# A gated FNet block on one core: the order of the side jobs around the first MLP1 units, earlier bias copies and an earlier load for MLP2, and one closing addition on GpSimd

## The chip, the cores and the metric

The kernel runs on one core of a Trainium2 chip. The metric is the device time of one execution in microseconds. Three runs of the kernel before are given, and one more execution was profiled.

## The reference

The input `x` has 2048 rows of 512. It is normalised by rows, goes through a Fourier mixing (real part of a two-sided DFT) and, beside that, through a two-layer MLP with squared ReLU; the MLP's output is passed through SiLU and gates the Fourier part, and `x` is added.

```python
xn = _layernorm(x)
a = jnp.einsum("bsd,ed->bse", xn, dft_hid_re)
b = jnp.einsum("bsd,ed->bse", xn, dft_hid_im)
s = jnp.einsum("ts,bse->bte", dft_seq_re, a) - jnp.einsum("ts,bse->bte", dft_seq_im, b)
h = jnp.einsum("bsd,df->bsf", xn, w1) + b1      # F = 1792
h = jnp.maximum(h, 0) ** 2
g = silu(jnp.einsum("bsf,fd->bsd", h, w2) + b2)
return x + s * g
```

## The kernel before

Every large product is in fp32 accuracy: an operand is split into a high part (`split_hi`, a copy on ScalarE, L125) and a low part (`split_lo`, a subtraction on VectorE, L128), and three matmuls, high·high, high·low and low·high, make one product (`PASSES`). On top of that, blocks of 2 by 2 are multiplied with seven products instead of eight (`PRODUCTS`), so each operand also needs sums of its blocks (`sums_a`, `sums_b`: three VectorE instructions, L257 to L269) ahead of the split. A tile's preparation is therefore a load (a DMA issued by SyncE, SP), sums on VectorE, a high split on ScalarE and a low split on VectorE.

The order on every engine is the order in which the Python code issues the instructions; nothing reorders them. The preparations are generators: each name such as `V6` or `x3` stands for one tile, and every mention of it in a table makes `go` run that tile's next step. The names that matter here: `x0` to `x7` are the token tiles of MLP1 (`tokens`: load, normalisation with two L610 instructions, sums, splits), `V2` to `V6` the first-layer weights that are made in place (`make_w1`: load, sums, splits), `m` the rows of statistics, `w` the second-layer weights (`make_w2`), `l4` and `l5` loads of second-layer weights, `h` the operands of MLP2 (`operand`: load, sums, splits), `y` and `p` operands and weights of the Y stage.

The stages follow each other on TensorE:

- up to 98 us: the sequence DFT of chunks 0 and 1 (`products`), whose results leave the four banks `pq1` through `last_out`;
- up to 335 us: chunks 2 to 7, 8 steps (c, j) of 42 matmuls each (L325). `EARLY` names the side steps behind each (c, j);
- up to 413 us: the Y stage, eight `YUnit`s with the hidden DFT (L704). `Y_SIDE` names two lists of side steps for each unit;
- up to 562 us: MLP1, 28 `HUnit`s H0 to H27 (L704), seven for each quarter c of the tokens. H6, for example, uses the weight of `V6`, and from H7 on the tiles `x2` and `x3` are used;
- up to 702 us: MLP2, 28 steps n of 42 matmuls (`outer`, L810), the first of them laid into H27, and the gate with the output.

In an `HUnit` the order on TensorE is: its product 1, the products 5 and 4 of the unit before, its products 7 and 6, product 3 of the unit before, its product 2. Product 3 goes into the bank (region B) in which product 5 lay, so it waits until VectorE has read that (`c22`, L774). `H_SIDE` gives three lists of side steps: the first is issued ahead of product 1, the second behind `c21` of the unit before, the third at the end. A side step on VectorE that stands in the first list thus stands ahead of `c22` in VectorE's queue, and one in the second list behind it. On VectorE a unit's own work is L774 twice and L789.

At the start of MLP2 two bias copies (`bias`, on ScalarE) put `b2` into the banks of products 2 and 4. In step n of MLP2 the operand `h(n+3)` gets its sums and then `h(n+2)` its split. `h2`, `h3` and all later operands lie in a buffer of the rotation `u` (three buffers, also used by the results of MLP1) or in `wd0`.

The tail computes the last quarter's four blocks, C11, C22, C12, C21: bias and sums of the products (`step`, L1035), SiLU on ScalarE, a product with the Fourier part (`times`, L857), an addition of `x` (`plus`, L862) and the store.

Of the kernel before, what the change touches and what calls it, by code (L numbers as in the profile page):

```python
# [11 lines left out]
ALU = mybir.AluOpType  # L12

P = 128
S, D, F = 2048, 512, 1792
NS, ND, NF = S // P, D // P, F // P
NJ, NP = NS // 2, NF // 2
# [3 lines left out]
NTC = S // TC  # L21
# [19 lines left out]
}  # L41

# [6 lines left out]
    (("x0",), ("k1",)),  # L49
    (("x1",), ()),  # L50
    (("V2", "x1", "x1", "m1"), ("x1", "V3", "x2")),
    (("x0", "x0", "V2", "V4", "V3"), ("x1", "x1", "x2")),
)


H_SIDE = {
    0: ((), ("V2",), ()),
    1: (("V4",), ("V3",), ("V5", "x3")),
    2: (("x2",), ("V4",), ("V6",)),
    3: (("V5",), ("V5",), ()),  # L60
    4: (("V6",), ("V6",), ("w4",)),
    5: ((), ("x2", "x3", "m2"), ("x4",)),
    6: (("x3",), ("x3",), ("x5",)),
    7: (("w4",), ("w4",), ("w5",)),
    8: ((), ("x4",), ()),
    9: (("x4",), ("x4",), ("x6",)),
# [10 lines left out]
    22: (("w1",), ("h0",), ("w2",)),  # L77
    23: ((), ("h1",), ("w3",)),
    24: (("w2",), ("w1",), ("w6", "h2")),
    25: (("w3",), ("w2",), ("l4",)),  # L80
    26: (("w6",), ("w3",), ("l5", "h3")),
    27: (("h2",), (), ()),
}
ACT_PAIR = (7, 10, 13, 15, 17, 18, 19, 20, 26)
O_SIDE = {0: (("h4",), ("h5",)), 1: ((), ("w6",))}
# [28 lines left out]
C21, C11, C22, C12 = range(4)  # L114
# [5 lines left out]
def fnet_gated_kernel(ctx, tc, x, xt, ct, wd, w1, w2, b1, b2, out):  # L120
    nc = tc.nc
# [8 lines left out]
    def split(*parts):  # L130
        split_hi(*parts)
        split_lo(*parts)

    def copy(to, src, scale=1.0):
        nc.scalar.activation(to, src, AF.Copy, scale=scale)
# [19 lines left out]
    def bank(tag, name):  # L155

        return acc.tile([P, 512], F32, tag=tag, name=name)

    def buf(tag, shape, name, dtype=F32):
        bufs = {"u": 3, "bn": 3, "sm": 3}.get(tag, 1)  # L160
        return pool.tile(shape, dtype, tag=tag, bufs=bufs, name=name)
# [109 lines left out]
    def sums_rows(t, r, turned=False):  # L271

        sums_a(t, r[:, C12:C12 + 1], r[:, C11:C22 + 1], r[:, C11], r[:, C21], turned)
# [75 lines left out]
    def go(*names):  # L349


        for v in names:
            if v[0] == "h" and int(v[1:]) >= NTC * NP:
                continue
            if v not in making:
                making[v] = makers[v[0]](int(v[1:]))
            next(making[v])
# [177 lines left out]
    def last_out(k, op):  # L535
        to = last.rearrange("p (h i m d t) -> p h d m i t", h=2, i=2, m=2, d=2)[:, k // 2, k % 2]
        op(to, accs[1][k].rearrange("p (m i t) -> p m i t", m=2, i=2))

    for k in range(3):
        last_out(k, nc.vector.tensor_copy)  # L540


    closing = None
    for n, s in enumerate(steps):
        c, j = s
        if j == 0:
            ms = {k: bank(tag, f"m{k}_{c}") for k, tag in
                  {1: "bb", 2: "b20", 6: "b21", 3: "b30", 5: "b31", 7: "b32", 4: ("ba", "bc")[c % 2]}.items()}
# [23 lines left out]
        if j == NJ - 1:  # L572
            e = buf("e", [P, 2048], f"c{c}")
# [9 lines left out]
    xT, W1, W2, fin, ready = {}, {}, {}, {}, {}  # L583
# [82 lines left out]

    def operand(n):

        if n < 2:
            x_, t = (buf(f"pq{n}{i}", [P, 4, 256], f"hr{n}_{i}") for i in range(2))  # L670
        else:
            e = buf("u" if n % 4 else "wd0", [P, 8, 256], f"hr{n}")
            x_, t = e[:, 4:8], e[:, 0:4]
        nc.sync.dma_start(x_, HD[divmod(n, NP)])
        yield
        sums_rows(t, x_)
        yield
        g = ready[n] = buf(("xc6", "xc7", "xc4")[n % 3], [P, 2, 7, 256], f"g{n}", F32R)
        for s, src in ((slice(0, 4), t), (slice(4, 7), x_[:, 0:3])) if n < 2 else ((slice(0, 7), e[:, 0:7]),):
            split(g[:, HI, s], g[:, LO, s], src)  # L680
        yield

# [5 lines left out]
    class Unit:  # L688

        def __init__(self, n):  # L690
            self.n = n
            self.at = {}
# [105 lines left out]
    def bias(m, n, cols=slice(0, 2)):  # L798

        m = m.rearrange("p (k e) -> p k e", k=2)[:, cols]  # L800
        b = BIASED[n] * 256
        copy(m, b2s[:, None, b:b + 256].to_broadcast([P, cols.stop - cols.start, 256]))
# [14 lines left out]
    def at(src, k):  # L817

        h, b = WHERE[k]
        return src.rearrange("(h k p) (b e) -> h b p k e", h=2, k=2, b=2)[h, b]  # L820
# [34 lines left out]
    def times(c, e, k, cols=slice(0, 2)):  # L855
        w = slice(cols.start * 256, cols.stop * 256)
        nc.vector.tensor_tensor(e[:, k, w], e[:, k, w], fin[c][k // 2][:, k % 2, w], op=ALU.mult)  # L857

    def plus(c, e, k, cols=slice(0, 2)):
        w = slice(cols.start * 256, cols.stop * 256)  # L860
        z = e[:, k, w]
        nc.vector.tensor_tensor(z, z, fin[c][2 + k // 2][:, k % 2, w], op=ALU.add)  # L862
        nc.sync.dma_start(at(out[c * TC:(c + 1) * TC], k)[:, cols], z.rearrange("p (k e) -> p k e", e=256))

    go("m0")
# [23 lines left out]
    for u in range(1, NC):  # L889
        n = 2 * u + 2  # L890
# [26 lines left out]
        before = unit  # L917


    for n in range(NTC * NP):  # L920
        unit = HUnit(n)
        first, second, later = H_SIDE.get(n, ((), (), ()))
        go(*first)
        unit.products(1)
        unit.seed("B", "A")
        before.c11()
        before.products(5)
        before.c22()
        before.products(4)
        before.c21()  # L930
        go(*second)
        unit.products(7)
        unit.m7()
        unit.products(6)
        unit.seed("C", "B")
        before.products(3)
        before.c12()
        unit.products(2)
        before.square()
        go(*later)  # L940
        before = unit

    class Banks(dict):

        def __init__(self, c):
            self.c = c

        def __missing__(self, k):
            tag = {1: "bb", 2: "b20", 6: "b21", 4: ("ba", "bc", "ba")[self.c], 7: ("bc", "b32", "b32")[self.c],
                   5: "b30", 3: "b31"}[k]  # L950
            self[k] = bank(tag, f"m{k}_o{self.c}")
            return self[k]

    ms = Banks(0)
    bias(ms[2], 2)
    bias(ms[4], 4)
    outer(ms[1], 1, 0)
    before.c11()
    before.products(5)
# [12 lines left out]
    for n in range(NTC * NP):  # L972
        c, p = divmod(n, NP)
        last = c == NTC - 1
        if n and not last and p == 0:

            ms = Banks(c)
            for k in (2, 4, 5):
                bias(ms[k], k)
        elif last and p == 0:  # L980

            ms = {k: bank(t, f"m{k}_last") for k, t in
                  {1: "b20", 2: "b21", 6: "b30", 7: "b31", 5: "bb", 3: "ba"}.items()}
            m4 = bank("bc", "m40_last"), bank("b32", "m41_last")
            bias(ms[5], 5)
            bias(m4[0], 4, slice(0, 1))
            bias(ms[2], 2)
            bias(m4[1], 4, slice(1, 2))

        def add(k, p):  # L990
            if last and k == 4:
                for i in range(2):
                    outer(m4[i], k, NP * c + p, (i,))
            else:
                outer(ms[k], k, NP * c + p)

        go(*O_SIDE.get(n, ((), ()))[0])
        if n == 1:
            for k, i in ((1, 1), (2, 1), (6, 1), (4, 1), (5, 0), (3, 0), (7, 1), (5, 1), (3, 1)):
                add(k, i)  # L1000
        elif n and (not last or p < REST):
            for k in ORDER if p else FIRST_LAST if last else FIRST:
                add(k, p)
        if n == 1:

            nc.scalar.activation(stats[:, 0, 0, 0:1], stats[:, 0, 0, 0:1], AF.Silu)
        go(f"h{n + 3}")
        if p == NP - 1 and not last:
            e = buf("e", [P, 4, 512], f"z{c}")
            list(combine(lambda k: halves(e[:, k]), ms))  # L1010
            done_next = c, e
        if c and not last and p in (3, 4):
            put(*done, p - 1)
        go(f"h{n + 2}", *O_SIDE.get(n, ((), ()))[1], f"h{n + 6}")
        if p == (3 if last else 5):
            load_fin(c)
        if p == NP - 1 and not last:
            done = done_next
        elif c:
            for k in ((2, 3), (0,), (1,), (), (), (), ())[p] if not last else ((), (0,), (1,), (2,), (3,), (), ())[p]:  # L1020
                finish(*done, k)


    e = buf("u", [P, 4, 512], f"z{c}")
    tail = NP - 1
    whole = slice(0, 512)
    w = [slice(i * 256, (i + 1) * 256) for i in range(2)]
# [6 lines left out]
    def step(to, a, b, op, w=whole):  # L1034
        nc.vector.tensor_tensor(e[:, to, w], a[:, w], e[:, b, w], op=op)  # L1035
# [25 lines left out]
    for f in range(REST, NP):  # L1061
        outer(m4[1], 4, NP * c + f, (1,))
    times(c, e, C12)
    step(C21, m4[1], C21, ALU.subtract, w[1])
    silu(e, C21, two)
    times(c, e, C21, one)
    plus(c, e, C21, one)
    times(c, e, C21, two)
    plus(c, e, C21, two)
    plus(c, e, C12)  # L1070


def _launch(arrays, out_shape):
# [40 lines left out]
```

## Time and profile before

| what | value |
|---|---|
| three runs | 708.91, 710.57, 710.85 us; median 710.57 us |
| profiled execution, own time | 709.49 us |
| profiled execution, span of its instructions | 707.7 us |
| TensorE busy with matmuls | 696.0 us (98%), 5440 matmuls |
| VectorE busy | 607.6 us (86%) |
| ScalarE busy | 357.0 us (50%) |
| granted TensorE clock | 0.999 |

The page of the profile gives busy time by engine, the chain of work that ended last and the costliest groups of instructions. The timeline lists instructions with their start, their duration and, in brackets, the idle time of the engine ahead of them and what ended it. "x12" means that twelve instructions of one kind that followed each other are merged into the row. Matmuls are pipelined: one lasts some 280 ns in the profile, while the next begins after 118 ns.

### The profile page before, as it was taken

Reading aid. Unit: us, or ns where it says so; the run is one execution under the profiler, and the core shown is the slowest. Engines: PE = TensorE matmul, PEld = TensorE weight load, DVE = VectorE, ACT = ScalarE, POOL = GpSimd, SP = SyncE. Lnnn points to the kernel's source line nnn. Section 1 sums busy time; section 2 is a strip of 40 time slices with the busy share of each in tenths; the row PEclk is TensorE's granted clock in tenths of the full one; section 3 lists DMA queues with packets and bytes.
Section 4 is the critical chain, followed back from the end, with each engine's and each line's share of the span. In section 5 each row is a group of like instructions: output and inputs, shape, how many; then the busy total and the mean of one; then the engine's idle time right before and its main releaser. Section 6 shows DMA issues by size and latency. Waiting matters only on the chain.

```text
span 707.7 us, 13133 instructions
## 1 busy us (share of the span) xinstructions
PE 696.0 (98%) x5440; PEld 671.6 (95%) x5440; DVE 607.6 (86%) x850; ACT 357.0 (50%) x471; POOL 5.2 (1%) x8
## 2 busy tenths in 40 slices
PE   9999999999999999999999999999999999999996
PEld 6778889999999999999999999999999999999996
DVE  7999779999989887888899699999649489989896
ACT  4446534444433333353455457677778754444441
POOL 0000000000000000000000000000000000101000
PEclk9999999999999999999999999999999999999999
DMA  8535755667575545286588444687426855767743
GB/s 302 189 112 188 280 193 206 244 225 266 189 273 211 181 145 179 90 283 229 176 294 273 155 167 161 215 338 259 163 114 221 316 184 192 188 204 191 238 151 119
DMA packets 50619, 146.88 MB, mean 208 GB/s; under 512 B 4864, under 2 KB 19200, under 8 KB 49152
## 3 DMA queue, kind: packets, MB, share of 16 engines
q1 hardware_dynamic: 43264, 126.13, 52.4%
q10 hardware_dynamic: 6208, 18.88, 6.8%
q0 software_dynamic: 1088, 1.05, 1.0%
q8 instruction: 42, 0.69, 0.4%
q14 instruction: 17, 0.14, 0.1%
HBM read 99.88 MB, written 46.15 MB: 206 GB/s over the span
## 4 chain that ended last, share of the span: by engine, by line
PE 90%; DVE 5%; ACT 2%; DMA 1%; issue 1%; ACTq 0%; DVEq 0%; SPq 0%
PE m L325 32%; PE m_o L810 14%; PE r_B L704 13%; PE r_A L704 8%; PE pq_b L340 7%; PE m_last L810 5%; PE r_C L704 4%; PE r_D L704 4%; PE pq_bb L340 1%; PE pq_ba L340 1%; PE pq_bc L340 1%; DMA hr<-hd 1%; DVE g L128 1%; DVE yg L128 1%; DVE c L306 1%
## 5 line engine op out<-in xcount | busy, mean ns | idle before, releaser
L325 PEld LDWEIGHTS m<-g,xc 128*128 128x128 f32 x2016 | 236.4, 188 | 1.3 <-DVE g L128 0.6
L325 PE MATMUL m<-g,xc 128*128 128x256 f32 x2016 | 237.0, 280 | 0.7 <-DVE g L128 0.4
L125 ACT ACTIVATE g<-u 128x1792 fp32r<-128x1792 f32 (+3 forms) x70 | 100.1, 1430 | 145.6 <-PE m L325 76.8
L128 DVE TENSOR_TENSOR g<-u,g 128x1792 fp32r<-128x1792 f32 (+3 forms) x70 | 117.5, 1679 | 26.7 <-ACT g L125 26.5
L810 PE MATMUL m_o<-w,g 128*128 128x256 f32 x882 | 106.1, 282 | 1.4 <-DVE g L128 1.0
L810 PEld LDWEIGHTS m_o<-w,g 128*128 128x128 f32 x882 | 105.5, 191 | 1.8 <-DVE g L128 1.2
L125 ACT ACTIVATE g<-hr 128x1792 fp32r<-128x1792 f32 (+2 forms) x30 | 47.9, 1603 | 50.7 <-PE m_o L810 31.2
L704 PE MATMUL r_B<-xT,w 128*128 128x256 f32 x504 | 69.6, 282 | 1.3 <-DVE h L774 1.3
L340 PE MATMUL pq_b<-g,xc 128*128 128x512 f32 x240 | 66.8, 397 | 0.3 <-ACT xc L125 0.2
L704 PEld LDWEIGHTS r_B<-xT,w 128*128 128x128 f32 x504 | 64.2, 190 | 1.5 <-DVE h L774 1.5
L128 DVE TENSOR_TENSOR g<-hr,g 128x1792 fp32r<-128x1792 f32 (+2 forms) x30 | 56.7, 1894 | 3.2 <-ACT g L125 3.2
L340 PEld LDWEIGHTS pq_b<-g,xc 128*128 128x128 f32 x240 | 43.8, 188 | 13.2 <-ACT xc L125 2.4
L704 PE MATMUL r_A<-xT,w 128*128 128x256 f32 x336 | 45.5, 283 | 0.6 <-DVE xT L128 0.6
L704 PEld LDWEIGHTS r_A<-xT,w 128*128 128x128 f32 x336 | 42.2, 190 | 1.2 <-DVE xT L128 1.0
L704 PE MATMUL r_B<-wdp,yg 128*128 128x256 f32 x288 | 37.5, 283 | 0.2 <-DVE y L714 0.2
L704 PEld LDWEIGHTS r_B<-wdp,yg 128*128 128x128 f32 x288 | 35.6, 190 | 0.6 <-DVE y L714 0.4
L810 PE MATMUL m_last<-w,g 128*128 128x256 f32 x294 | 35.3, 282 | 0.0
L810 PEld LDWEIGHTS m_last<-w,g 128*128 128x128 f32 x294 | 35.2, 191 | 0.0
L257 DVE TENSOR_TENSOR u<-u 128x512 f32<-128x512 f32 x48 | 32.9, 685 | 0.7 <-DMA u<-in_ct 0.7
L128 DVE TENSOR_TENSOR yg<-yraw,yg 128x1792 fp32r<-128x1792 f32 x13 | 26.2, 2022 | 5.5 <-ACT yg L125 5.4
L306 DVE TENSOR_TENSOR c<-m,c 128x512 f32<-128x512 f32 x42 | 27.2, 685 | 1.8 <-PE m L325 1.0
L125 ACT ACTIVATE yg<-yraw 128x1792 fp32r<-128x1792 f32 x13 | 22.1, 1700 | 6.7 <-DVE yraw L266 5.2
(171 smaller groups left out, 863.5 us busy)
## 6 DMA issues: line engine op xcount, KB each, us to landing
u<-in_ct SPq DMA_DIRECT2D x63, 512.0 KB, 3.6
hd<-h ACTq DMA_DIRECT2D x28, 512.0 KB, 4.4
hr<-hd SPq DMA_DIRECT2D x28, 512.0 KB, 3.7
wdp<-wdd SPq DMA_DIRECT2D x8, 896.0 KB, 7.3
yraw<-pqd SPq DMA_DIRECT2D x13, 512.0 KB, 4.7
pqd<-c SPq DMA_DIRECT2D x6, 1024.0 KB, 4.3
y<-y ACTq DMA_DIRECT2D x8, 512.0 KB, 5.0
fin<-y SPq DMA_DIRECT2D x16, 256.0 KB, 4.6
```

Source lines behind the costliest of these rows:

```text
L125: nc.scalar.activation(hi, src, AF.Copy)
L128: nc.vector.tensor_tensor(lo, src, hi.bitcast(F32), op=ALU.subtract)
L257: nc.vector.tensor_tensor(t[:, 0:2], r[:, 0:1].to_broadcast([P, 2, 256]), r[:, 1:3], op=ALU.add)
L306: nc.vector.tensor_tensor(part_(to), m, part_(frm), op=op)
L325: nc.tensor.matmul(ps[:, d], w[:, a_, d * P:(d + 1) * P], halves(mv(b_)), start=first and d == 0 and (a_, b_) == (HI, HI), stop=last and ( ...
L340: nc.tensor.matmul(accs[c][k], w, part[c, j][:, b_, 2 * h:2 * h + 2], start=j == 0 and h == 0 and (a_, b_) == (HI, HI), stop=j == NJ - 1 a ...
L704: nc.tensor.matmul(self.region(REGION[k]), w, mv, start=i == 0 and k in (1, 7), stop=i == len(ops) - 1, skip_group_check=True)
L810: nc.tensor.matmul(m[:, i * 256:(i + 1) * 256], ready[n][:, a_, H_SLOT[a], i * P:(i + 1) * P], W2[p][:, b_, b], start=p == 0 and i == 0 an ...
```

## The change

- `last_out` for chunk 1: of three copies that VectorE made in the order 0, 1, 2, two (2 and 0) go to ScalarE, ahead of its next split, and VectorE keeps 1.
- `EARLY`: the splits of `y0` and `y1` are issued one step (c, j) later, and with them the load of `y2`.
- `Y_SIDE`: in the last Y unit `x1` is split ahead of the sums of `V2`, and the sums of `V3` follow the load of `V4`.
- `H_SIDE`: in H0 to H6 the sums of `x2`, `V5`, `V6` and the normalisation and sums of `x3` move from the first lists to the second ones or to other units. `V6` is split in H5 instead of H4, `x2` in H4 instead of H5; `x3` is loaded one unit earlier, ahead of `V5`; the loads of `m2`, `x4` and `w4` move too.
- MLP2: the bias copies for products 2 and 4 are issued in H27 ahead of ScalarE's square of H26; `h3` is loaded one unit earlier, ahead of `l4` and `l5`, into a buffer pair of its own (`pq00`, `pq01`); the split of `h2` stands ahead of the sums of `h3`.
- Tail: the addition of `x` for block C12 goes from VectorE, where it was last, to GpSimd, directly behind its product; its store is then issued ahead of those of C21.

```diff
-    (7, 1): ("p2",), (7, 2): ("p2", "y0"), (7, 3): ("y0", "y2", "p3"), (7, 4): ("p3", "y1"), (7, 5): ("y1",),
+    (7, 1): ("p2",), (7, 2): ("p2",), (7, 3): ("y0", "p3"), (7, 4): ("y0", "y2", "p3"), (7, 5): ("y1", "y1"),
...
-    (("x0", "x0", "V2", "V4", "V3"), ("x1", "x1", "x2")),
+    (("x0", "x0", "x1", "x1", "V2"), ("V4", "V3", "x2")),
...
-    0: ((), ("V2",), ()),
-    1: (("V4",), ("V3",), ("V5", "x3")),
-    2: (("x2",), ("V4",), ("V6",)),
-    3: (("V5",), ("V5",), ()),
-    4: (("V6",), ("V6",), ("w4",)),
-    5: ((), ("x2", "x3", "m2"), ("x4",)),
-    6: (("x3",), ("x3",), ("x5",)),
+    0: ((), ("V2", "x2"), ("x3",)),
+    1: (("V4",), ("V3",), ("V5",)),
+    2: ((), ("V4", "V5"), ("V6",)),
+    3: ((), ("x3", "V5"), ("m2",)),
+    4: ((), ("V6", "x2"), ("x4",)),
+    5: ((), ("V6", "x3"), ("w4",)),
+    6: ((), ("x3",), ("x5",)),
...
-    25: (("w3",), ("w2",), ("l4",)),
-    26: (("w6",), ("w3",), ("l5", "h3")),
+    25: (("w3",), ("w2",), ("h3", "l4")),
+    26: (("w6",), ("w3",), ("l5",)),
...
-    for k in range(3):
-        last_out(k, nc.vector.tensor_copy)
+    for k, op in ((2, copy), (0, copy), (1, nc.vector.tensor_copy)):
+        last_out(k, op)
...
-        if n < 2:
-            x_, t = (buf(f"pq{n}{i}", [P, 4, 256], f"hr{n}_{i}") for i in range(2))
+        apart = n in (0, 1, 3)
+        if apart:
+            x_, t = (buf(f"pq{n % 3}{i}", [P, 4, 256], f"hr{n}_{i}") for i in range(2))
...
         before.c12()
+        if n == NTC * NP - 1:
+            ms = Banks(0)
+            for k in (2, 4):
+                bias(ms[k], k)
         unit.products(2)
         before.square()
...
-    bias(ms[2], 2)
-    bias(ms[4], 4)
...
+        if not n:
+            go("h2")
         go(f"h{n + 3}")
...
-        go(f"h{n + 2}", *O_SIDE.get(n, ((), ()))[1], f"h{n + 6}")
+        go(*[f"h{n + 2}"][:n], *O_SIDE.get(n, ((), ()))[1], f"h{n + 6}")
...
     times(c, e, C12)
+    plus(c, e, C12, eng=nc.gpsimd)
     step(C21, m4[1], C21, ALU.subtract, w[1])
...
     plus(c, e, C21, two)
-    plus(c, e, C12)
```

More of the change, by code (lines that the diff above doesn't have):

```diff
@@ L678, in operand @@
         g = ready[n] = buf(("xc6", "xc7", "xc4")[n % 3], [P, 2, 7, 256], f"g{n}", F32R)
-        for s, src in ((slice(0, 4), t), (slice(4, 7), x_[:, 0:3])) if n < 2 else ((slice(0, 7), e[:, 0:7]),):
+        for s, src in ((slice(0, 4), t), (slice(4, 7), x_[:, 0:3])) if apart else ((slice(0, 7), e[:, 0:7]),):
             split(g[:, HI, s], g[:, LO, s], src)
@@ L857, in times, with plus @@
         nc.vector.tensor_tensor(e[:, k, w], e[:, k, w], fin[c][k // 2][:, k % 2, w], op=ALU.mult)
-    def plus(c, e, k, cols=slice(0, 2)):
+    def plus(c, e, k, cols=slice(0, 2), eng=None):
         w = slice(cols.start * 256, cols.stop * 256)
         z = e[:, k, w]
-        nc.vector.tensor_tensor(z, z, fin[c][2 + k // 2][:, k % 2, w], op=ALU.add)
+        (eng or nc.vector).tensor_tensor(z, z, fin[c][2 + k // 2][:, k % 2, w], op=ALU.add)
         nc.sync.dma_start(at(out[c * TC:(c + 1) * TC], k)[:, cols], z.rearrange("p (k e) -> p k e", e=256))
@@ L917, in fnet_gated_kernel, with __init__, __missing__ @@
         before = unit
+    class Banks(dict):
+        def __init__(self, c):
+            self.c = c
+        def __missing__(self, k):
+            tag = {1: "bb", 2: "b20", 6: "b21", 4: ("ba", "bc", "ba")[self.c], 7: ("bc", "b32", "b32")[self.c],
+                   5: "b30", 3: "b31"}[k]
+            self[k] = bank(tag, f"m{k}_o{self.c}")
+            return self[k]
     for n in range(NTC * NP):
@@ L941, in fnet_gated_kernel @@
         before = unit
[L943 to L954, printed above, removed]
-    bias(ms[2], 2)
-    bias(ms[4], 4)
     outer(ms[1], 1, 0)
```

## The prediction

> **What bounds the kernel now.** I read the page first, then TensorE's waits, then the timeline around each wait.
>
> ```profile
> PE 696.0 (98%) x5440; PEld 671.6 (95%) x5440; DVE 607.6 (86%) x850; ACT 357.0 (50%) x471; POOL 5.2 (1%) x8
> ...
> L325 PE MATMUL m<-g,xc 128*128 128x256 f32 x2016 | 237.0, 280 | 0.7 <-DVE g L128 0.4
> ```
>
> TensorE (PE) is the bound; the change takes no matmul away, so all it can win are PE's stops and the tail behind the last matmul. The second row gives the size of a stop: 2016 matmuls in 237.0 us are one each 0.118 us, but one lasts 0.28 in the profile, so that an idle time in the rows is understated by 0.16. The longest stops with a releaser (their idle time, how many, the longest):
>
> ```profile
> PE r_B L704 <- DVE h L774: 1.3, 1, 1.3
> ...
> PE m_o L810 <- DVE g L128: 1.0, 1, 1.0
> PE r_A L704 <- DVE xT L128: 0.6, 1, 0.6
> ```
>
> These three, and three shorter ones whose rows stand below, belong to places that the change edits. Behind a stop the second matmul also comes late: six of them take 0.98 us at 450.39 (row below), as against the 0.87 of others, so 0.1 more. A stop costs its idle time, 0.16 and 0.1.
>
> **Copies of chunk 1 (`last_out`).**
>
> ```profile
> 98.42 1.88 DVE L537 COPY plain<-pq_b 128x512 f32<-128x512 f32 x3
> 98.67 1.71 ACT L125 ACTIVATE g<-u 128x1792 fp32r<-128x1792 f32 x1 [3.81 <-DVE u L259]
> ...
> 100.45 5.73 PE L325 MATMUL m<-g,xc 128*128 128x256 f32 x47 [0.29 <-DVE plain L537]
> ...
> 105.88 2.02 DVE L128 TENSOR_TENSOR g<-u,g 128x1792 fp32r<-128x1792 f32 x1 [0.39 <-ACT g L125]
> ```
>
> PE waits for the third of three VectorE copies, that of bank 2. ScalarE (ACT) has sat idle 3.81 us ahead of 98.67, so two copies fit there before its split, and VectorE's single one ends near 99.1, ahead of its use. The stop of 0.29 + 0.16 + 0.1, about 0.53, goes. What is late next: the low split at 105.88 follows VectorE's own chain and ends at 107.90 whatever PE does; PE, 0.5 earlier, wants it near 107.84 and stands some 0.15. Gain **0.4** (0.2 to 0.53).
>
> **The Y operands in `EARLY`.**
>
> ```profile
> 311.32 0.96 DVE L128 TENSOR_TENSOR yg<-yr,yg 128x768 fp32r<-128x768 f32 x1 [1.47 <-ACT yg L125]
> ...
> 313.72 2.02 DVE L128 TENSOR_TENSOR g<-u,g 128x1792 fp32r<-128x1792 f32 x1
> ...
> 315.79 4.47 PE L325 MATMUL m<-g,xc 128*128 128x256 f32 x36 [0.37 <-DVE g L128]
> ```
>
> The half split of `y0` (0.96) stands on both engines ahead of the split of g(7,4), for which PE stops. Behind it, g ends near 314.2, before PE's 315.2. The moved work is 4 half splits within some 15 us in which every step leaves VectorE about 1 us; the load of `y2` waits until 320.4, is needed at 329, and holds one load of `p3` on SP for less than a microsecond, which is used at 335. Gain 0.37 + 0.16 + 0.1 = **0.6** (0.4 to 0.65).
>
> **Y7 and H0 to H6.** Here the answer is not the stop that goes, but VectorE's queue.
>
> ```profile
> 406.89 2.08 DVE L128 TENSOR_TENSOR xT<-x0e,xT 128x768 fp32r<-128x768 f32 x2
> 408.89 0.69 DVE L263 TENSOR_TENSOR w1raw<-w1raw 128x512 f32<-128x512 f32 x1
> ...
> 410.41 0.68 DVE L263 TENSOR_TENSOR w1raw<-w1raw 128x512 f32<-128x512 f32 x1
> ...
> 412.08 0.88 PE L704 MATMUL r_A<-xT,w 128*128 128x256 f32 x4
> ...
> 413.56 0.50 PE L704 MATMUL r_A<-xT,w 128*128 128x256 f32 x2 [0.61 <-DVE xT L128]
> ...
> 414.64 2.48 DVE L610 TENSOR_TENSOR xr<-xr,rows 128x1024 f32<-128x1024 f32 x2
> ...
> 417.04 0.42 DVE L714 TENSOR_TENSOR y<-r_B,y 128x256 f32<-128x256 f32 x1
> ...
> 417.90 2.02 DVE L128 TENSOR_TENSOR w<-w1raw,w 128x1792 fp32r<-128x1792 f32 x1
> ...
> 419.83 0.69 DVE L263 TENSOR_TENSOR w1raw<-w1raw 128x512 f32<-128x512 f32 x1
> ...
> 427.21 0.48 DVE L774 SCALAR_TENSOR_TENSOR h<-r_B,b1s,h 128x256 f32<-128x256 f32 x1
> ...
> 428.92 2.02 DVE L128 TENSOR_TENSOR w<-w1raw,w 128x1792 fp32r<-128x1792 f32 x1
> ...
> 444.64 1.59 PE L704 MATMUL r_A<-xT,w 128*128 128x256 f32 x12
> ...
> 450.39 0.98 PE L704 MATMUL r_B<-xT,w 128*128 128x256 f32 x6 [1.32 <-DVE h L774]
> ...
> 452.57 0.30 PEld L704 LDWEIGHTS r_A<-xT,w 128*128 128x128 f32 x2 [0.23 <-DVE xT L128]
> ```
>
> H0 starts at 412.08 and stands four matmuls later, until 413.56: 1.0 + 0.1 = 1.1. In the changed order the splits of `x1` run on VectorE at 408.89, where the weight sums are now, and that goes whole. The stop in H6 (1.32 + 0.16 + 0.1 = 1.6) is `c22`, held in VectorE's queue behind the normalisation and sums of `x3`; with the 0.3 at 452.57 (low split of `x3`) 3.0 stands to be won.
>
> But the same work has to pass VectorE. Its costs from start to next start are: split pair of a token tile 2.00 (408.89 − 406.89), weight or token sums 1.52 (410.41 − 408.89), normalisation 2.40 (417.04 − 414.64), Y7's two 0.86 (417.90 − 417.04), weight split 1.93 (419.83 − 417.90), a unit's own three 1.71 (428.92 − 427.21). From 408.89 the changed queue is: `x1` split, two weight sums, `x2` normalisation, Y7's two, `V2` split, `x2` sums, `V4` sums, H0's three, `V3` split: 2.00 + 3.04 + 2.40 + 0.86 + 1.93 + 1.52 + 1.52 + 1.71 + 1.93 = 16.9, to 425.8. Then four units' three, `V4`, `V5` splits, `V5`, `V6` sums, `x3` normalisation, `x2` split: 6.84 + 3.86 + 3.04 + 2.40 + 2.00 = 18.1, to 443.9. There the split of `V6` begins; it ends at 446.0 (2.02).
>
> H6 needs that split: its product 1 takes the low part of `V6` at the third matmul. H6 starts in the second half of the row at 444.64, at 445.36; 1.1 earlier that is 444.25, its third matmul 444.5. So a new stop of 1.5 + 0.1 stands at H6's start, where before only `c22` waited; part of it may fall on H5's product 3, without a change in the sum. Even with no backlog the split of `V6` would be late: it follows `c22` of H4 in H5's list and leaves VectorE about 0.3 too late. Behind it `c22` of H5 and the `x3` split pass in time. Net 3.0 − 1.6 = **1.4** (0.5, if VectorE idles a microsecond for a load; 2.6, if no backlog forms).
>
> The loads moved here: `x3`'s load waits on SP for Y7's store, and `V5`'s and `V6`'s loads stand behind it (rival 2).
>
> **Start of MLP2.**
>
> ```profile
> 559.34 1.12 ACT L135 ACTIVATE m_o<-b2s 128x512 f32<-128x512 f32 x2 [0.40 <-ACT h L793]
> ...
> 560.00 1.69 PE L810 MATMUL m_o<-w,g 128*128 128x256 f32 x12 [0.44 <-ACT m_o L135]
> ...
> 564.49 1.71 ACT L125 ACTIVATE g<-hr 128x1792 fp32r<-128x1792 f32 x1 [0.40 <-ACT h L793]
> ...
> 567.79 0.69 DVE L263 TENSOR_TENSOR hr<-hr 128x512 f32<-128x512 f32 x1 [6.99 <-DMA hr<-hd]
> ...
> 569.32 2.02 DVE L128 TENSOR_TENSOR g<-hr,g 128x1792 fp32r<-128x1792 f32 x1
> ...
> 571.40 28.82 PE L810 MATMUL m_o<-w,g 128*128 128x256 f32 x239 [0.95 <-DVE g L128]
> ```
>
> The bias copies (1.12) go ahead of the square of H26, whose 1.06 us and store then lie between: ScalarE reaches them at 557.8, PE needs the first at 559.4. The stop of 0.44 + 0.16 + 0.1 = 0.7 goes; the delayed store is that of an operand used 28 units on. At 571.40 PE waits for the low split of `h2`, which stood in VectorE's queue behind the sums of `h3`; those idled 6.99 us for a load. With `h2` first, the split can run at 566, behind its high half (564.49 + 1.71, 0.7 earlier), and PE wants it at 569.6: 0.95 + 0.16 + 0.1 = 1.2 goes. What is late next, `h3`, has its load moved from behind `l5` to ahead of `l4`, 16 us earlier, and PE needs it at 574.6, two microseconds behind its split. Gain **1.9** (1.2 to 1.9).
>
> **Tail.**
>
> ```profile
> 703.39 1.03 DVE L862 TENSOR_TENSOR z<-z,fin 128x256 f32<-128x256 f32 x2
> ...
> 639.15 1.21 POOL L845 DMA_DIRECT2D z<-in_x  x1 [28.84 <-DVE z L857]
> ...
> out<-z SPq DMA_DIRECT2D x5, 256.0 KB, 2.1
> ...
> out<-z SPq DMA_DIRECT2D x2, 128.0 KB, 1.7
> ```
>
> VectorE's last two additions end at 704.42; without C12's 0.68 the last ends near 703.8, and the last store is then one of 128 KB (1.7 to landing) instead of 256 KB (2.1): up to 0.9 less. No row shows an addition on GpSimd (POOL). From below it is VectorE's 0.68; from above I put 2.2, near twice POOL's 1.21 for another kind. C12's product is done at 701.9; with 1.2 its store leaves at 703.2 and the later ones behind it in time (0.9). With 2.2 they queue behind it on SP, and the gain is gone (−0.3). Whether POOL's addition stops VectorE's four of 0.42 that run in the same time, no row shows either: with 1.2 that eats the 0.9. I take the middle of 0 and 0.9, **0.4** (−1.0, with 2.2 and stopping, to 0.9).
>
> The Trainium skill speaks against the edit twice. "SBUF — State Buffer", section "SBUF: two separate sides", states that GpSimd and VectorE share one port pair, locked for a whole instruction, and that a VectorE operation with two SBUF inputs is blocked by a GpSimd one that reads SBUF. By that rule the edit is worth 0 instead of 0.4 and the sum 0.4 less. No run shows it so far. "GPSIMD Engine Reference", section "Instruction dispatch", states some 6 us for the first call of freshly loaded code; that is rival 3.
>
> **Sum.** 0.4 + 0.6 + 1.4 + 1.9 + 0.4 = 4.7 us. The profiled execution took 709.49, 1.08 below the median of the three runs; the four times average 709.96, and from that I take the 4.7: 705.3 us.
>
> **Rivals.**
>
> 1. VectorE stays the bound through H0 to H6 and something in it, such as a load, gives back that stage's 1.4 and the tail: 0.4 + 0.6 + 1.9 − 0.4 = 2.5, 707.5 us. For it: the queue has no idle time from 408.89 to 446. Against: loads there landed long before use. Chance 0.12.
>
> 2. Slower. `x3`'s load is issued when Y7's store has landed, and `V5`'s load behind it.
>
> ```profile
> y<-y ACTq DMA_DIRECT2D x1, 512.0 KB, 5.4
> ...
> hd<-h ACTq DMA_DIRECT2D x1, 512.0 KB, 12.1
> ...
> w1raw<-in_w SPq DMA_DIRECT2D x1, 512.0 KB, 4.4
> ```
>
> Y7's store took 5.4 with a load issued just ahead of it; the 12.1 is a store behind two large loads. Issued at 419.1, plus 0.4 for `x3`'s issue and 4.4 for the load, `V5` has landed by the 429.6 at which VectorE wants it if the store takes no more than about 5.7. With 12.1 VectorE stands 6.4 us, straight into H3 to H6: 4.7 − 6.4 = −1.7, 711.7 us. Against: in the changed order no load is issued near that store. Chance 0.05.
>
> 3. POOL's first addition starts some 6 us late, for code that is not there yet (one more instruction stands ahead of it in POOL's queue and waits for nothing). C21's stores queue behind C12's: the tail loses 5 instead of winning 0.4, 4.7 − 5.4 = −0.7, 710.7 us. Against: that instruction can run right behind POOL's last DMA, 57 us earlier. Chance 0.06.
>
> 4. The changed order isn't what runs. The built order of instructions shows each move; chance 0.01.
>
> **How the numbers follow.** Forecast 0.76. About 0.3% (2.1 us) is what a measurement of this kernel tells from no change. The forecast's own bounds are a gain of 0.2 + 0.4 + 0.5 + 1.2 − 1.0 = 1.3 and of 0.53 + 0.65 + 2.6 + 1.9 + 0.9 = 6.6, 708.7 and 703.4; rivals 1 lies inside, 2 and 3 outside, with 0.11. Faster: most of the forecast and two thirds of rival 1, 0.81. Same: the forecast's lower end, the rest of rival 1, rival 3: 0.13. Slower: rival 2 and a little for two misses together, 0.06.
>
> **What would show it.** Right: no stop at 100, 315, 413, in H27 and at step 2 of MLP2; a stop of 1 to 2 us for the low split of `V6` (`w`, L128) at H6's start; VectorE without idle time from Y7 to H6. Wrong: a VectorE wait for `w1raw`, a POOL addition over 2 us, or the last four VectorE operations stretched beside it.

## The result, and the profile after

The changed kernel takes 705.96 us (median of six, 705.75 to 707.13), the kernel before 709.87 on the same chips: a ratio of 0.9949 [0.9935, 0.9964], 3.6 us less by that ratio and 3.9 by the medians. Forecast were 705.3 us and a range of 703.4 to 708.7; the result lies inside, 0.7 above the forecast. The profiled execution of after is the slowest of the six, 707.13 with a span of 705.4; the table further down therefore uses a second profile (`e1_again`, 705.77) beside it.

The page and the waits of TensorE (idle time, how many, the longest) of after; the lines of the program lie one lower than before (L774 is now L775):

```profile
PE 695.8 (99%) x5440; PEld 671.7 (95%) x5440; DVE 606.8 (86%) x848; ACT 357.9 (51%) x474; POOL 6.5 (1%) x9
```

```profile
PE r_A L705 <- DVE w L128: 1.3, 1, 1.3
...
PE r_B L705 <- DVE h L775: 0.8, 1, 0.8
PE r_B L705 <- DVE y L715: 0.2, 1, 0.2
```

The six stops of the prediction are gone. At the places of four of them, at 100 us, at 315 us and twice at the start of MLP2, TensorE's rows now show no idle time, and the split of `h2` runs at 565.13, directly behind its high half:

```profile
98.00 12.21 PE L325 MATMUL m<-g,xc 128*128 128x256 f32 x101
...
305.80 11.36 PE L325 MATMUL m<-g,xc 128*128 128x256 f32 x96
...
558.98 1.60 PE L811 MATMUL m_o<-w,g 128*128 128x256 f32 x12
...
561.13 14.13 PE L811 MATMUL m_o<-w,g 128*128 128x256 f32 x118
...
565.13 2.03 DVE L128 TENSOR_TENSOR g<-hr,g 128x1792 fp32r<-128x1792 f32 x1 [4.73 <-ACT g L125]
```

Two long stops stand in the list of waits, one of them forecast. That is its first row: H6 waits for the low split of V6. The timeline of after, TensorE and then VectorE:

```profile
443.00 1.11 PE L705 MATMUL r_A<-xT,w 128*128 128x256 f32 x8
445.43 0.74 PE L705 MATMUL r_A<-xT,w 128*128 128x256 f32 x4 [1.32 <-DVE w L128]
```

```profile
406.12 2.08 DVE L128 TENSOR_TENSOR xT<-x0e,xT 128x768 fp32r<-128x768 f32 x2
...
425.79 0.48 DVE L775 SCALAR_TENSOR_TENSOR h<-r_C,b1s,h 128x256 f32<-128x256 f32 x1 [0.16 <-PE r_C L705]
...
443.36 2.02 DVE L128 TENSOR_TENSOR w<-w1raw,w 128x1792 fp32r<-128x1792 f32 x1
```

Eight matmuls from 443.00 make the next one due at 443.94; it starts at 445.43, 1.49 late, and the one behind it loses 0.1. Between 406.12 and 443.36 VectorE's rows show one idle time, 0.16 us: the queue that the prediction added up.

The second stop was not forecast:

```profile
537.69 0.69 DVE L257 TENSOR_TENSOR w2raw<-w2raw 128x512 f32<-128x512 f32 x1 [1.89 <-DMA w2raw<-in_w]
...
539.22 0.48 DVE L775 SCALAR_TENSOR_TENSOR h<-r_B,b1s,h 128x256 f32<-128x256 f32 x1
...
539.75 0.98 PE L705 MATMUL r_B<-xT,w 128*128 128x256 f32 x6 [0.76 <-DVE h L775]
```

In H24 the sums of `w2` stand on VectorE ahead of `c22` of H23 and wait for their load. TensorE stops for 0.93 + 0.1, and loses 0.5 more in H25 to H27, since VectorE's rows from 537.69 to 555 are again without idle time.

The tail of after:

```profile
698.93 0.68 DVE L858 TENSOR_TENSOR z<-z,fin 128x512 f32<-128x512 f32 x1
...
699.54 0.43 DVE L1039 TENSOR_TENSOR z<-m_last,z 128x256 f32<-128x256 f32 x1
699.70 1.26 POOL L863 TENSOR_TENSOR z<-z,fin 128x512 f32<-128x512 f32 x1 [56.62 <-DVE z L858]
699.88 1.35 DVE L858 TENSOR_TENSOR z<-z,fin 128x256 f32<-128x256 f32 x1
...
702.07 0.42 DVE L863 TENSOR_TENSOR z<-z,fin 128x256 f32<-128x256 f32 x1
```

GpSimd's addition takes 1.26 us and starts 0.09 after its product. VectorE's product beside it takes 1.35 instead of 0.41.

### The profile page after: what moved, and what is told of

Its sections match the earlier page's. It is cut to its first block, busy times and chain, and to the rows that moved or that the text cites. A ratio compares the mean times of both kernels' runs of the same rounds, so it can differ in the third digit from the quotient of the medians.

```text
span 705.4 us, 13138 instructions
## 1 busy us (share of the span) xinstructions
PE 695.8 (99%) x5440; PEld 671.7 (95%) x5440; DVE 606.8 (86%) x848; ACT 357.9 (51%) x474; POOL 6.5 (1%) x9
## 4 chain that ended last, share of the span: by engine, by line
PE 93%; DVE 4%; DMA 1%; ACT 1%; issue 1%; DVEq 0%; ACTq 0%
PE m L325 33%; PE m_o L811 15%; PE r_B L705 12%; PE r_A L705 8%; PE pq_b L340 8%; PE m_last L811 5%; PE r_C L705 4%; PE r_D L705 4%; PE pq_ba L340 2%; PE pq_bb L340 1%; PE pq_bc L340 1%; DMA w2raw<-in_w 1%; DVE c L306 1%; DVE yg L128 0%; DMA x<-in_x 0%
```

## The experiments

My theories: (1) VectorE's queue from 409 us on sets the stop of H6; the rival was that only the place of V6's split in its list counts. (2) In the tail GpSimd and VectorE exclude each other; the rival was that GpSimd takes work off the bound. (3) The late load of `w2` is chance; the rival was that the change makes it late.

**The changed kernel again.** No edit.

> The changed kernel once more, for a second profile. In the first one TensorE stops 0.9 us at 538.7, in H24, because c22 stands behind the sums of w2, whose load (issued at 531.2) took 6.46 us to land, and VectorE stays late by 0.1 to 0.2 us in each of H25, H26 and H27: 1.5 us in all. Theory chance: the load's time varies, and most executions do not have this; then the profile shows the load at some 4.3 us, no stop in H24, and an execution of about 705.7 us. Rival: the change itself makes that load late; then the stop is there again and the execution takes about 707. Both expect the stop of 1.5 to 1.6 us at 443.8 for the low split of V6.

705.83 us (705.66 to 707.39; 0.9952 [0.994, 0.9965]); four executions of five lie within 705.66 to 706.11. The load of `w2` and the store that is issued 0.2 us behind it, first in after (load issued at 531.20), then in this profile (531.38); the columns are count, size and us to landing:

```profile
w2raw<-in_w SPq DMA_DIRECT2D x1, 512.0 KB, 6.5
hd<-h ACTq DMA_DIRECT2D x1, 512.0 KB, 6.4
```

```profile
w2raw<-in_w SPq DMA_DIRECT2D x1, 512.0 KB, 4.3
hd<-h ACTq DMA_DIRECT2D x1, 512.0 KB, 5.4
```

With 4.3 there is no stop in H24 to H27, and that is worth 1.5 us. Of the fourteen profiles of this study, before and after included, eleven show 4.2 to 4.4 and three 6.5 to 6.9, at the same distance from the store beside it, and the store is late with the load (5.3 to 5.5, or 6.4 to 6.8). The same program shows both, so the change by itself doesn't make the load late. Why it falls into two groups is open. The stop of V6 is the same in both profiles.

**VectorE relieved in H2, H3, H4.** A unit in `ACT_PAIR` leaves bias, maximum and square of its blocks C21 and C22 to ScalarE.

```diff
-ACT_PAIR = (7, 10, 13, 15, 17, 18, 19, 20, 26)
+ACT_PAIR = (2, 3, 4, 7, 10, 13, 15, 17, 18, 19, 20, 26)
```

> The changed kernel with H2, H3 and H4 added to the units whose closing work ScalarE shares: VectorE is spared 0.85 us in each of them (1.72 against 0.87 from start to start), 2.55 in all, ahead of the split of V6. Theory queue: what makes the low split of V6 late is the gapless row of VectorE work from 409 us; then the low split begins as soon as its high half is done (about 441.9), the stop of 1.6 at 443.8 shrinks to 0.1 to 0.5, and the kernel gains 1.1 to 1.5 us on the changed one. Rival place: the split stands too late in its list, behind the high half on ScalarE, and relief elsewhere does not help: no gain, and ScalarE's additional 1 us per unit delays the copies that TensorE needs, a loss of 0.2 to 0.5.

705.77 us (0.995 [0.9936, 0.9963]): the 1.1 to 1.5 us of the queue theory did not come; nothing is gained, as the rival said, though only in part for its reason. VectorE's row and ScalarE's rows:

```profile
443.55 2.03 DVE L128 TENSOR_TENSOR w<-w1raw,w 128x1792 fp32r<-128x1792 f32 x1 [2.07 <-ACT w L125]
```

```profile
439.72 1.06 ACT L794 ACTIVATE h<-h 128x1024 f32<-128x1024 f32 x1
...
441.82 1.70 ACT L125 ACTIVATE w<-w1raw 128x1792 fp32r<-128x1792 f32 x1
```

VectorE is free 2.07 us ahead of the low split, as the queue theory said. But H3's longer closing work stands on ScalarE ahead of the high split of V6, which starts at 441.82 instead of 440.35 (`e1_again`). The relief was handed on to ScalarE, and this run doesn't decide between the two theories.

**Relieved in H2 and H4 only.**

```diff
-ACT_PAIR = (7, 10, 13, 15, 17, 18, 19, 20, 26)
+ACT_PAIR = (2, 4, 7, 10, 13, 15, 17, 18, 19, 20, 26)
```

> The changed kernel with H2 and H4 alone added to the units whose closing work ScalarE shares. In e2_relief VectorE was free 2.07 us ahead of the low split of V6, but the longer square of H3 (1.06 instead of 0.63, with 0.7 for the LOWER blocks) stood on ScalarE ahead of the high split of V6 and made it 1.5 us later. The squares of H2 and H4 do not stand there. Theory queue: VectorE gains 1.7 us ahead of the low split, the high half ends at 441.9 as in the changed kernel, the low split begins there instead of at 443.4, and the stop of 1.6 shrinks to 0.2 to 0.5: 704.5 to 704.8 us. Rival place: whatever leaves VectorE's queue, the low split begins at 443.4; no gain.

704.93 us (0.9943 [0.9931, 0.9956]). VectorE's row, and TensorE's wait in the list of waits:

```profile
442.49 2.03 DVE L128 TENSOR_TENSOR w<-w1raw,w 128x1792 fp32r<-128x1792 f32 x1 [0.61 <-ACT w L125]
```

```profile
PE r_A L705 <- DVE w L128: 0.5, 1, 0.5
```

The stop shrinks from 1.49 to 0.63, and TensorE is 1.0 us earlier behind H6. That settles it for the queue; what is left, a little more than the 0.2 to 0.5 expected, now ends with ScalarE's high half.

**Relieved in H0 only.**

```diff
-ACT_PAIR = (7, 10, 13, 15, 17, 18, 19, 20, 26)
+ACT_PAIR = (0, 7, 10, 13, 15, 17, 18, 19, 20, 26)
```

> The changed kernel with H0 alone added to the units whose closing work ScalarE shares: VectorE is spared 0.85 us at 422, 21 us ahead of the low split of V6. In the profile of the changed kernel the only idle time of VectorE between 406 and 447 is 0.16 us ahead of 425.8, where it waits for TensorE (product 4 of H1). Theory queue, with that place as its start: the 0.85 turns into idle time there, and the stop at 443.8 stays 1.5 to 1.6 long. Rival: the queue is one from 409 on; then the stop shrinks by the 0.85, as H2 and H4 took 0.9 of it in e5_relief_h2_h4.

One execution, 706.11 us. VectorE's rows, then TensorE's:

```profile
424.70 0.48 DVE L775 SCALAR_TENSOR_TENSOR h<-r_B,b1s,h 128x256 f32<-128x256 f32 x1 [0.82 <-ACT h L794]
425.33 0.48 DVE L775 SCALAR_TENSOR_TENSOR h<-r_C,b1s,h 128x256 f32<-128x256 f32 x1 [0.15 <-PE r_C L705]
...
427.45 2.03 DVE L128 TENSOR_TENSOR w<-w1raw,w 128x1792 fp32r<-128x1792 f32 x1 [0.91 <-ACT w L125]
```

```profile
423.71 0.87 PE L705 MATMUL r_B<-xT,w 128*128 128x256 f32 x6
...
437.49 0.98 PE L705 MATMUL r_B<-xT,w 128*128 128x256 f32 x6 [0.71 <-DVE h L775]
...
445.97 0.74 PE L705 MATMUL r_A<-xT,w 128*128 128x256 f32 x4 [1.32 <-DVE w L128]
```

The 0.85 spared turns into 0.82 of idle time. The first row names H0's longer square on ScalarE as what ended it, but the product that this row reads ended on TensorE at 424.58 (423.71 + 0.87), only 0.1 before VectorE starts, and the next row waits 0.15 for TensorE, as it does in after at 425.79. So VectorE has caught up with TensorE there, and the queue that matters begins at 425. That V6's stop stays (1.48 long) doesn't show this by itself, because of a second idle time that was not expected: H0's longer square on ScalarE delays the high split of V4, VectorE loses 0.91 behind that place, and TensorE has a new stop of 1.0 at 436.5.

**The side jobs alone, on the kernel before.** Its `Y_SIDE` line and `H_SIDE` rows 0 to 6 become those of the change, the rest stays.

> The kernel before with only the new order of the side jobs in Y7 and H0 to H6. The prediction's term was 1.4 (0.5 to 2.6): the stops at 412.6 (1.1), 448.8 (1.6) and 452.6 (0.3) go, one of 1.6 comes for the low split of V6 at H6's start. Theory queue: gain 1.2 to 1.4, the new stop at 444.9 to 446.5 is 1.5 to 1.6 long although the copies of chunk 1 and the Y operands are not changed. Rival: in the changed kernel the stop is there because TensorE comes 0.8 us earlier by those two edits; then it is only 0.8 here and the gain 2.1.

708.83 us (0.9991 [0.9982, 1.0]), 0.4 under the kernel before where 1.2 to 1.4 were expected. The stop for V6's low split is 1.49 long here too, so it doesn't hang on TensorE being early; the stage itself gains 1.15, near what was expected. Half of it is given back at the start of MLP2; there VectorE and TensorE show:

```profile
567.14 0.69 DVE L263 TENSOR_TENSOR hr<-hr 128x512 f32<-128x512 f32 x1 [7.59 <-DMA hr<-hd]
...
570.74 4.47 PE L810 MATMUL m_o<-w,g 128*128 128x256 f32 x36 [1.55 <-DVE g L128]
```

Before, these waits were 6.99 and 0.95. The load of `h3` lands 0.65 earlier while TensorE comes 1.25 earlier, so 0.6 of the gain is waited away.

**The MLP2 part alone, on the kernel before.** The bias copies in H27, `apart`, the split of `h2` first, and `H_SIDE` rows 25 and 26.

> The kernel before with only the MLP2 part: bias copies in H27, h3's load ahead of l4 and l5 in a buffer of its own, the split of h2 ahead of the sums of h3. The prediction's term was 1.9 (1.2 to 1.9): the stops at 559.3 (0.7) and 570.2 (1.2) go and nothing new comes. Rival: with TensorE 2 us later here than in the changed kernel nothing else may differ; but if h3's earlier load is what makes w2's load or l4 late, a stop in H24 to H27 shows here too and the gain is 0.5 to 0.9.

707.95 us (0.9985 [0.9972, 0.9998]), by the medians 1.3 under the kernel before, with a term of 1.9 forecast; seven of eleven executions lie at 707.44 to 708.15, four at 709.2 to 710.15. In the profile, one of the four, the two stops are gone (0.69 and 1.21 us), and the late load of `w2` is there:

```profile
540.41 0.69 DVE L257 TENSOR_TENSOR w2raw<-w2raw 128x512 f32<-128x512 f32 x1 [2.05 <-DMA w2raw<-in_w]
...
542.48 0.97 PE L705 MATMUL r_B<-xT,w 128*128 128x256 f32 x6 [0.93 <-DVE h L775]
```

The load was issued at 533.8, in H22, and the first load that this part moves stands in H25, so that doesn't make it late. With TensorE 2.7 us later than in after the stop is no shorter (0.93 of idle time, 0.76 there), because the load's issue comes 2.6 us later as well.

**C12's addition on VectorE, in the same place.**

```diff
-    plus(c, e, C12, eng=nc.gpsimd)
+    plus(c, e, C12)
```

> The changed kernel with the addition of x for C12 on VectorE, in the same place directly behind its product. Theory lock: GpSimd's 1.26 us stop VectorE's product beside it (1.35 instead of 0.41), so that GpSimd's addition costs VectorE 0.9 where the addition itself costs 0.69; then the last addition ends about 0.2 to 0.3 us earlier after the last matmul (2.99 us in the changed kernel), the last store stays one of 128 KB, and the kernel gains 0.2 to 0.3. Rival: VectorE's queue is what sets the end and GpSimd takes 0.69 off it: a loss of 0.4 to 0.7.

705.56 us (0.9945 [0.9933, 0.9958]), without an execution over 705.95. VectorE's rows:

```profile
697.37 0.68 DVE L858 TENSOR_TENSOR z<-z,fin 128x512 f32<-128x512 f32 x1
698.09 0.69 DVE L863 TENSOR_TENSOR z<-z,fin 128x512 f32<-128x512 f32 x1
698.70 0.42 DVE L1039 TENSOR_TENSOR z<-m_last,z 128x256 f32<-128x256 f32 x1
699.03 0.42 DVE L858 TENSOR_TENSOR z<-z,fin 128x256 f32<-128x256 f32 x1
...
700.27 0.42 DVE L863 TENSOR_TENSOR z<-z,fin 128x256 f32<-128x256 f32 x1
```

From the end of the last matmul to VectorE's last addition it is 2.75 us, against 2.99 in after; from its start to the end of the span 5.90, against 6.14.

**C12's addition on VectorE, last, as before the change.**

```diff
-    plus(c, e, C12, eng=nc.gpsimd)
...
     plus(c, e, C21, two)
+    plus(c, e, C12)
```

> The changed kernel with the tail of the kernel before: C12's addition on VectorE, behind those of C21, its store of 256 KB the last. Theory lock: the tail from the last matmul to the end is as long as in the changed kernel, within 0.1 us, since the gain of the smaller last store (0.4) and the delay by GpSimd (0.3) cancel; against e3_tail_vector it is 0.3 to 0.4 longer. Rival (the addition on GpSimd is worth the 0.4 of the prediction): 0.4 longer than in the changed kernel.

705.88 us (0.9946 [0.9933, 0.996]); 2.65 and 6.23 by the same measure, exactly those of the kernel before. So of the 0.33 that can be had here (6.23 to 5.90), GpSimd leaves 0.09. All of it comes from the order, not from the engine.

**The sums of `w2` behind `c22`.**

```diff
-    24: (("w2",), ("w1",), ("w6", "h2")),
+    24: ((), ("w1", "w2"), ("w6", "h2")),
```

> The changed kernel with the sums of w2 moved from the first list of H24 (ahead of c22 of H23) to the end of its second list. Theory chance: in most executions the load lands in time and nothing changes (705.7), and the slowest executions, which showed 707 to 707.4 in one run of five, are gone: all within 0.6 us. Rival: the executions at 707 have another cause; they stay, one or two in five. Against: the split of w2 now has the sums less far ahead of it; if that is late, a stop in H25 of up to 0.5.

706.57 us (0.9963 [0.9951, 0.9976]), all within 706.24 to 706.86. The executions at 707 are gone, but by the trace the kernel is 0.75 longer than `e1_again`, 0.4 of it in H25. VectorE's row, and TensorE's:

```profile
537.01 0.48 DVE L775 SCALAR_TENSOR_TENSOR h<-r_B,b1s,h 128x256 f32<-128x256 f32 x1 [1.14 <-PE r_B L705]
```

```profile
544.30 0.98 PE L705 MATMUL r_B<-xT,w 128*128 128x256 f32 x6 [0.20 <-DVE h L775]
```

In the first list the sums filled a wait of VectorE for TensorE; now it idles 1.14 us there, and the work missing from that gap is late in H25 to H27. This profile had the late load (6.9), but it landed at 538.2 and the sums start at 540.72 without an idle time, so the 0.75 doesn't come from VectorE waiting for it.

**The same, with H23 and H24 relieved; then the parts together.** `e10_w2_relief` is that edit with 23 and 24 added to `ACT_PAIR`. `e11_best` adds 2 and 4 and C12's addition on VectorE behind its product. `e12_relief_tail` is `e11_best` without the edits of 23, 24 and row 24.

> The changed kernel with the sums of w2 at the end of H24's second list, as in e6_w2_sums, and with H23 and H24 added to the units whose closing work ScalarE shares. In e6_w2_sums VectorE stood idle 1.14 us ahead of c22 of H23, since the sums no longer filled that time, and c22 of H24, H25 and H26 came 0.2 to 0.5 late behind a gapless row of work. Theory: the 1.7 us that VectorE is spared make up for it; no stop in H24 to H27, no execution over 706.3, median 705.5 to 705.8. Rival: ScalarE's longer squares of H23 and H24 delay the high splits of w1 and w2 by 1.1; then a stop of 0.5 to 1 in H25 or H26 and a median of 706.3 or more.

> e10_w2_relief with H2 and H4 sharing too (e5_relief_h2_h4: 0.9 to 1.0) and C12's addition on VectorE directly behind its product (e3_tail_vector: 0.24). If the parts add: 705.6 - 0.9 - 0.24, some 704.5 us, all executions within 0.7. Rival: TensorE, 0.9 earlier at H7, runs into the next late step, and less than half of it is left: 705.0 or more.

> The changed kernel with only H2 and H4 sharing and C12's addition on VectorE behind its product; the sums of w2 stay where they are. If the parts add: 705.8 - 0.9 - 0.24, some 704.6 us in most executions, and one in five some 1.5 us above for the load of w2. Rival as for e11_best.

| kernel | median, us | executions | ratio to before |
|---|---|---|---|
| e10_w2_relief | 705.82 | 705.43 to 706.19 | 0.9933 [0.9912, 0.9954] |
| e11_best | 704.81 | 704.61 to 704.98 | 0.9919 [0.9898, 0.994] |
| e12_relief_tail | 704.57 | 703.68 to 706.35 | 0.992 [0.9895, 0.9945] |

`e10_w2_relief` has the median of the changed kernel and a narrower spread: by its trace it still loses 0.3 from H25 on, the relief of H23 and H24 takes back the rest. The parts add to within 0.3 us (704.5 and 704.6 expected for the other two). `e12_relief_tail` is fastest in its good executions, but they spread over 2.7 us, more than the 1.5 of the late load; its one profile (704.16) had the early load, so what the slow ones had is not shown. `e11_best` pays 0.3 in H25 for executions that all lie within 0.4 us. Both medians lie 1.0 to 1.4 us under those of the changed kernel (705.83 and 705.96, on other chips).

## Why the prediction was right, point by point

The terms, with what TensorE's start times show in `e1_again` against before:

| step | forecast | measured |
|---|---|---|
| copies of chunk 1 | 0.4 | 0.28 |
| Y operands in `EARLY` | 0.6 | 0.64 |
| Y7, H0 to H6 | 1.4 | 1.12 |
| start of MLP2 | 1.9 | 1.91 |
| tail | 0.4 | 0.09 |
| sum | 4.7 | 4.04 |

The copies and `EARLY` were not run alone; their rows rest on the traces of the whole change. Of the 4.7, 0.7 is missing: 0.3 in the tail, 0.3 in Y7 to H6 and 0.1 at the copies. The profiled executions lie 3.7 apart (709.49 and 705.77). The 0.3 between these 3.7 and the 4.04 has no place in the change: in stretches of the chunk stage 42 matmuls take 4.95 us in `e1_again` and 4.90 in before, and the same pace changes elsewhere the other way.

- **Copies.** The stop went (0.53). The low split behind it, due at 105.88 to 107.90, ran at 105.98 to 108.01 (after), and TensorE stood 0.25 for it instead of 0.15.
- **Y7 to H6.** The place, the length and the cause of the new stop came out as added up: 1.5 + 0.1 forecast, 1.49 + 0.1 measured. The stops that went are 1.1, 1.58 and 0.29; 0.16 more was lost in H5, where product 3 of H4 waits in the same queue; the prediction had allowed for a shift there, not for an addition. The last 0.1 went in steps of less than 0.1. The 2.6 without a backlog came in no run: 1.7 us taken off VectorE (`e5_relief_h2_h4`) got 1.0 of the stop back.
- **MLP2.** Both stops went, by 0.7 and 1.2. `e7_sides_alone` adds what the prediction didn't say: this part also keeps the gain of H0 to H6, of which the old start of MLP2 would have waited 0.6 away.
- **Tail.** This is the mis-sized term. I took the middle of 0 and 0.9; measured is 0.09. One of the signs of being wrong came with it: of the last four VectorE operations one is stretched. By the rule quoted there from the Trainium skill ("SBUF — State Buffer", "SBUF: two separate sides") it would have been 0, and the trace agrees: VectorE's product with two SBUF inputs starts at 699.88 while GpSimd runs and ends at 701.23, 0.27 behind GpSimd's end, and with the addition on VectorE (`e3_tail_vector`) the same product takes 0.42. The step that reads one input from PSUM (L1039 at 699.54) takes its usual 0.43 although GpSimd runs beside it from 699.70. GpSimd's price of 1.26 lay near the lower of my two cases (1.2), but even so the stopping ate the gain.
- **Rivals.** Rival 1 (707.5) is wrong in its place, H0 to H6, where no load made VectorE wait; but the profiled execution with a late load came to 707.13 in the same way, 100 us later in the program, in a queue that I had not added up. The others between 707.0 and 707.4 were not profiled. Rival 2: Y7's store took 2.8, but `x3`'s load was issued only at 421.29 and V5's at 421.70, which took 6.4; it landed at 428.15 for sums at 428.86. With 0.7 us to spare it was nearer than my 0.05 made it. Rival 3: GpSimd's addition started 0.09 us behind its product, with no sign of the 6 us that the Trainium skill gives for a first call ("GPSIMD Engine Reference", "Instruction dispatch"); the instruction that stands ahead of it (`MODIFY_POOL_CONFIG`) ran at 642.6, behind GpSimd's last DMA and 57 us earlier, as the prediction had argued. What a first call costs without such a lead, no run here shows.

## What to carry to other kernels

When jobs are only moved, add up the queue that has to take them, from its last idle time on: work spared before that point turns into idle time, and work given to a second engine counts in that engine's queue ahead of what the first one waits for. A stop that is taken away early in a program is worth its length only as far as the next step that is tied to a load. A second engine for the last operations of a tail gains little if the two exclude each other, as they did here (0.09 of 0.33 us); try the order on one engine first.

## What the runs showed of the hardware

- GpSimd's addition of 128x512 (1.26 us) held a VectorE operation with two SBUF inputs until it was done (1.35 us instead of 0.42); one with an input in PSUM took its usual 0.43 with 0.27 of it beside GpSimd's addition.
- A load of 512 KB beside a store of the same size issued 0.2 us later took 4.2 to 4.4 us (eleven profiles) or 6.5 to 6.9 (three), with nothing between, in the same place of nearly equal programs.
